# The first two slots' rows asked for ahead of q, k and v, and ten memsets instead of seven between indirect writes, in an attention and mixture-of-experts kernel

## The chip, the cores and the metric

The kernel runs on one core of one Trainium2 chip. The metric is device time in microseconds (us) of one execution; lower is better. A core has five instruction queues that run at the same time, each in its own order: TensorE (PE in the profile; its weight loads are listed as PEld), VectorE (DVE), ScalarE (ACT), GpSimd (POOL) and SyncE (SP). SP computes nothing here: it asks for transfers between the chip's memory and the core's. A request that has to wait holds up every request behind it on the same queue.

## The reference, cut to what matters

Dilated and sliding-window attention over 8 batches, 8 heads, 576 positions and 64 features, then a dropless mixture of 8 experts over the 4608 tokens that come out, each token going to the one expert with the largest logit.

```
scores = where(mask[h], q @ k.T / sqrt(64), -1e9)     # h < 4: 32 newest keys; h >= 4: every 4th of 128
x      = softmax(scores) @ v                          # (8, 8, 576, 64) -> (4608, 512)
e      = argmax(x @ w_gate);  gate = softmax(x @ w_gate)[e]
y      = gate * (relu(x @ w1[e]) @ w2[e])             # w1: 512 x 1024, w2: 1024 x 512, fp32
```

## The kernel before, in words

**Attention** goes through 16 pairs p (batch b = p // 2, head type ty = p % 2), two units each. For a pair SP loads q and k into a tile `raw` (3 buffers, `load_whole`, L379), DVE transposes them into `qT` and `kT` (L538, L549), and SP loads v into one of two tiles with a single buffer each: v0 for even pairs in one request (L405, shown as v_71 in the order), v1 for odd pairs in 13 requests (L429, v_72). A unit is then: PE `scores` (L595), DVE masking (L611) and row minimum (L623), ACT exponentials (L629), DVE reciprocal (L640, L642), POOL normalisation (L646), PE transposes `weights` (L657, three groups of three, over two small PSUM banks), ACT or DVE copies to `eT` (L878), PE `xo` (L676), and a copy to `xT`.

**Routing** of a batch b follows its two pairs. PE computes `lp` and `logits` (L976), DVE chooses the expert (`choose`, L988 to L994, which frees the bank that `logits` took), counts (`front`, L998), PE ranks (L1007, L1010), DVE makes the row numbers `idx` (L1022), PE and ACT or DVE turn x into token rows (`xrow` L939, `rows` L950), and POOL writes the rows into `bucket` in memory, sorted by expert, with five indirect writes (L493). After the batches 1, 2, 4 and 7 DVE also makes tables (L1142 and on) that tell which rows the next slots hold.

**Experts** work on slots of up to 128 rows of one expert. For slot j SP asks for the rows (`fetch_x`: four requests for `x`, L1379, and one for the gates `gt`, L1384), which waits until the writes of the batches so far have landed in `bucket`. It asks for the weights (`fetch_w`, L1401) only where the expert is another than two slots before. DVE transposes x to `xt` (L1407), PE runs the first layer `ph` (L1415, 8 pieces of 4 matmuls, 32 in all) and the second `py` (L1431, 8 matmuls), ACT and DVE evict (L1426, L1436), and POOL scatters the result to the output (L1456). Slots 0 and 1 can start after batch 1, slots 2 to 5 after batch 2. What is left over per expert goes through 14 small slots (`ph_s`, `h_s`, `py_s`, L1518 to L1545) near the end.

**The order** on all five engines is made by a planner before the program is built (class `Plan`). Each piece of work is a step with guessed durations, with steps it comes after, rings of buffers it takes, and a rank. The planner repeatedly takes, among the steps that could start within 0.25 of the earliest one, the one with the lowest rank, and appends its instructions to its engine. Where PE would idle in the attention part it puts in filler matmuls on a constant tile (L714, `<-idle`), as many as fit the idle time it expects. Between two indirect transfers that follow each other on POOL it puts IDLE one-column memsets of a tile that nobody reads (L722), and counts on 0.21 for each. The engines then run these fixed orders; only semaphores decide when.

Of the kernel before, what the change touches and what calls it, by code (L numbers as in the profile page):

```python
# [63 lines left out]
STEP_W = 1.0  # L64
ROUTE = 5.0

IDLE = 7

MOVED = 3.0
MOVED_S = 1.5  # L70
# [3 lines left out]
WHOLE = 14  # L74

QUADS = 4

BY_PE = 0
RUN, LONG = S * 4 // 128, S // 16
# [2 lines left out]
class Ring:  # L82


    def __init__(self, bufs):
        self.bufs, self.holds = bufs, []
# [19 lines left out]
class Step:  # L106
    def __init__(self, engines, us, emit, after, takes, uses, rank, moved, dense, slow, dmas):
        self.engines = (engines,) if isinstance(engines, str) else engines
        self.us = dict.fromkeys(self.engines, us) if isinstance(us, float) else us
        self.emit, self.after, self.rank, self.moved = emit, after, rank, moved  # L110
        self.slow, self.dmas = slow, dmas
        self.takes, self.uses = takes, [*takes, *uses]
        self.end, self.dense, self.on = None, dense, None
        for h in self.uses:
            h.left += 1


class Plan:
# [18 lines left out]

    APART = 0.21 * IDLE

# [66 lines left out]
    def write(self):  # L206
# [8 lines left out]
        while open_:  # L215
            found = []
            for s in open_:
                free = [h.ring.free_at() for h in s.takes]
                if None not in free:
                    found.append(min(  # L220
                        (self.could(s, free, e) for e in s.engines),
                        key=lambda f: f[0] + s.us[f[2]] + self.COSTS.get(f[2], 0.0),
                    ))
            soon = min(f[0] for f in found) + self.SOON
            at, _, e, s = min((f for f in found if f[0] <= soon), key=lambda f: (f[1], f[0]))
            if e == "PE" and self.fill and not self.filled(s):
                idle, cold = at - self.free[e] - self.SLACK, self.slowed(at) > 1.0
                us = self.FILL * self.slowed(self.free[e])
# [3 lines left out]
            if e == "PE":  # L232
                at = max(at, self.free[e])
# [95 lines left out]
def kernel(  # L329
# [11 lines left out]
    packed, at = _constants()  # L341
# [364 lines left out]
    def hold(name):  # L706
        return Hold(ring[name])
# [12 lines left out]
    def pass_time():  # L720
        for _ in range(IDLE):
            nc.gpsimd.memset(still, 0.0)  # L722
# [11 lines left out]
    def attention():  # L734
# [12 lines left out]
        for p, (b, ty) in enumerate(pairs):  # L747
# [60 lines left out]
            for n in range(0 if p < BY_PE else 2):  # L808
                for g in range(2 if p < WHOLE else 1):
# [10 lines left out]
                    )  # L820
            quad = p < QUADS
            for hp in range(2):
# [807 lines left out]
    def moe():  # L1630
# [10 lines left out]
        asked = {}  # L1641

        def ask(j):
            known, sent = slot_known[j]
            hx = hold("x") if j < SURE else None
            asked[j] = (
                add("SP", 3.5, lambda e: fetch_x(j), after=[known, *sent],
                    takes=[hx] if hx else (), rank=900.0 + j, moved=1.4, dmas=5),
                hx,
            )  # L1650

        for j in range(3):
            ask(j)
        for j in range(SURE):
            known, sent = slot_known[j]
            D = {}
# [181 lines left out]
```

## Time and profile before

| | us |
|---|---|
| median of 3 runs (lowest, highest) | 781.12 (780.31, 782.7) |
| the profiled execution, whole | 781.74 |
| its span, first to last instruction | 780.0 |
| PE busy in the span | 742.8 |
| POOL busy in the span | 193.5 |

The whole time of the profiled execution is 1.74 us above its span; that part lies outside of the instructions. The profiled execution is 0.62 us above the median of the runs. The rows of the trace further down show, for an engine, when a group of instructions started, how long it took, its line, operation, output and input, its count, and in brackets how long the engine sat idle just before and what ended that. A matmul in fp32 appears as two records in the trace, so that `x18` is nine filler matmuls, while the order counts instructions. For SP a row shows when requests were issued, not when they landed.

### The profile page before, as it was taken

The page shows a single profiled execution, that of the slowest core. Times are in us where ns is not written, and L with a number is a line of the kernel's source. Part 1 is how long each engine was busy: PE and PEld are TensorE (multiplying, and loading weights), DVE is VectorE, ACT ScalarE, POOL GpSimd, SP SyncE. Part 2 cuts the span into 40 slices and gives each one's busy share as a digit, 9 for nine tenths or more (in the row PEclk, how much of TensorE's full clock was granted, in tenths as well). Part 3 has the DMA queues.
Part 4 walks back from the last instruction along what each step waited for, and adds up shares of the span by engine and source line. Part 5 has one row for each costly group of instructions (what it writes and reads, how often), then busy time and mean ns, then how long its engine had stood idle before and what let it go on. Part 6 is the DMA issues. An engine that isn't in the chain of part 4 may idle for free.

```text
span 780.0 us, 21889 instructions
## 1 busy us (share of the span) xinstructions
PE 742.8 (95%) x8406; PEld 562.4 (72%) x8406; DVE 257.6 (33%) x718; ACT 265.2 (34%) x868; POOL 193.5 (25%) x641
## 2 busy tenths in 40 slices
PE   5879989999999999999999999999999999999996
PEld 5768878868787776776776776777776776766664
DVE  7958858678857740710000000000000000000000
ACT  2766756576747754211111111111111111111100
POOL 1314343425253434260100100211221111102101
PEclk9989999999999999999999999999999999999999
DMA  9878775969997979799629684727678166099660
GB/s 274 301 224 272 229 239 137 361 190 323 260 268 178 298 226 350 262 387 323 214 47 314 201 258 100 254 51 250 196 261 299 35 226 261 22 316 351 257 222 30
DMA packets 140399, 180.68 MB, mean 232 GB/s; under 512 B 68764, under 2 KB 90014, under 8 KB 139776
## 3 DMA queue, kind: packets, MB, share of 16 engines
q1 hardware_dynamic: 132864, 159.00, 64.1%
q0 software_dynamic: 6272, 19.43, 6.5%
q8 instruction: 68, 1.11, 0.6%
q10 hardware_dynamic: 1152, 0.78, 0.4%
q14 instruction: 43, 0.35, 0.1%
HBM read 252.03 MB, written 19.95 MB: 349 GB/s over the span
## 4 chain that ended last, share of the span: by engine, by line
PE 80%; issue 8%; DMA 6%; DVE 3%; ACT 2%; POOL 1%; SPq 0%; POOLq 0%; DVEq 0%; ACTq 0%
PE ph L1415 27%; PE py L1431 25%; PE scores L595 6%; PE xo L676 6%; PE weights L657 4%; DMA qT<-in_moe_w_dram 4%; PE py_s L1545 3%; PE ph_s L1518 3%; PE weights L714 3%; PE xrow L939 2%; PE lp L962 1%; DMA raw<-in_k_dram 1%; DMA x<-bucket 1%; PE logits L976 1%; ACT eT L878 1%
## 5 line engine op out<-in xcount | busy, mean ns | idle before, releaser
L1415 PEld LDWEIGHTS ph<-xt,w 128*128 128x128 f32 x2112 | 243.2, 192 | 15.7 <-issue 14.6
L1415 PE MATMUL ph<-xt,w 128*128 128x128 f32 x2112 | 252.5, 277 | 0.0
L1431 PE MATMUL py<-w,h 128*128 128x512 f32 x528 | 236.5, 594 | 0.6 <-ACT h L1426 0.6
L1431 PEld LDWEIGHTS py<-w,h 128*128 128x128 f32 x528 | 96.0, 190 | 101.3 <-issue 100.8
L629 ACT ACTIVATE e<-e,lo 128x96 f32<-128x96 f32 x288 | 103.5, 363 | 19.6 <-DVE lo L623 19.6
L1407 DVE STREAM_TRANSPOSE xt<-x 128x512 f32<-128x512 f32 x30 | 21.3, 711 | 243.7 <-PE ph L1415 240.4
L1456 POOL DMA_INDIRECT out_dram<-y,to x30 | 29.5, 984 | 251.7 <-ACT y L1436 249.2
L646 POOL TENSOR_TENSOR e<-e,rec 128x864 f32<-128x864 f32 x32 | 52.3, 1633 | 141.1 <-DVE rec L642 112.6
L1426 ACT ACTIVATE h<-ph 128x512 f32<-128x512 f32 x63 | 37.6, 597 | 142.6 <-PE ph L1415 141.8
L1436 ACT ACTIVATE y<-py,gt 128x512 f32<-128x512 f32 x30 | 20.6, 687 | 157.8 <-PE py L1431 150.3
L595 PE MATMUL scores<-kT,qT 32*64 32x96 f32 (+1 forms) x2160 | 56.2, 259 | 12.0 <-issue 7.4
L595 PEld LDWEIGHTS scores<-kT,qT 32*64 32x64 f32 (+1 forms) x2160 | 49.1, 139 | 18.5 <-issue 14.3
L722 POOL MEMSET still<- 128x1 f32 x504 | 51.4, 102 | 25.0
L629 ACT ACTIVATION_READ_ACCUMULATOR e<-e,lo 128x1 f32 x288 | 54.4, 189 | 0.0
L493 POOL DMA_INDIRECT bucket<-rows,idx x40 | 39.2, 980 | 60.9 <-issue 16.9
L676 PEld LDWEIGHTS xo<-eT,v 96*64 96x64 f32 x1280 | 40.9, 138 | 12.3 <-issue 4.5
L657 PE MATMUL weights<-cst,e 128*96 128x128 f32 x288 | 45.1, 282 | 4.5 <-ACT eT L878 2.1
L611 DVE SCALAR_TENSOR_TENSOR e<-scores,cst 128x384 f32<-128x384 f32 (+1 forms) x128 | 45.5, 395 | 10.0 <-PE scores L595 9.0
L676 PE MATMUL xo<-eT,v 96*64 96x64 f32 (+1 forms) x1280 | 45.9, 225 | 3.0 <-issue 2.6
L878 ACT COPY eT<-weights 96x384 f32<-96x384 f32 x88 | 39.9, 480 | 22.8 <-PE weights L657 16.1
L657 PEld LDWEIGHTS weights<-cst,e 128*96 128x96 f32 x288 | 30.2, 129 | 17.2 <-issue 6.8
L1511 DVE STREAM_TRANSPOSE own<-own 128x128 f32<-128x128 f32 x14 | 4.3, 304 | 99.3 <-DMA own<-bucket 99.3
(168 smaller groups left out, 566.5 us busy)
## 6 DMA issues: line engine op xcount, KB each, us to landing
w<-in_moe_w_dram SPq DMA_DIRECT2D x66, 2048.0 KB
raw<-in_moe_w_dram SPq DMA_DIRECT2D x42, 1024.0 KB
qT<-in_moe_w_dram SPq DMA_DIRECT2D x28, 512.0 KB
w<-in_moe_w_dram SPq DMA_DIRECT2D x8, 1024.0 KB
raw<-in_q_dram SPq DMA_DIRECT2D x14, 576.0 KB
raw<-in_k_dram SPq DMA_DIRECT2D x14, 576.0 KB
x<-bucket SPq DMA_DIRECT2D x120, 64.0 KB
v<-in_v_dram SPq DMA_DIRECT2D x7, 864.0 KB
```

The source lines that it names most:

```text
L493: nc.gpsimd.indirect_dma_start(out=bucket, out_offset=bass.IndirectOffsetOnAxis(ap=idx, axis=0), in_=rows, in_offset=None, bounds_check=NR ...
L595: nc.tensor.matmul(two[r][QB * half : QB * half + QB, KB * c : KB * c + KB], lhsT=qT[:, QB * n : QB * n + QB], rhs=kt[:, QB * n : QB * n + ...
L611: nc.vector.scalar_tensor_tensor(out=e[p, c0 : c0 + w], in0=sc[r][p, a : a + w], scalar=-SCALE, in1=m[p, a : a + w], op0=OP.mult, op1=OP.add,)
L629: nc.scalar.activation(out=ev[:, c], in_=ev[:, c], func=AF.Exp, bias=lo[:, c : c + 1], scale=-1.0, accum_out=den[:, c : c + 1],)
L646: nc.gpsimd.tensor_tensor(out=ev, in0=ev, in1=rec.unsqueeze(2).broadcast_to([128, NC, KB]), op=OP.mult)
L657: nc.tensor.transpose(tp[0:KB, c], ev[:, 3 * g + c], ident)
L676: nc.tensor.matmul(xo[DH * r : DH * r + DH, g, lo - half_s * g : hi - half_s * g], lhsT=v0[:, hd, n] if ty == 0 else v1[:, n, hd], rhs=eT[ ...
L722: nc.gpsimd.memset(still, 0.0)
L878: copier(e)(S_["eT"][:, 3 * g : 3 * g + 3], S_["w", g][0:KB, 0:3])
L1415: nc.tensor.matmul(ph[:, f % 4], lhsT=w1s[j % 2][:, c, 128 * f : 128 * f + 128], rhs=xt[:, c], start=c == 0, stop=c == 3,)
L1426: nc.scalar.activation(to, ph, AF.Relu)
L1431: nc.tensor.matmul(py, lhsT=h[:, f], rhs=w2s[j % 2][:, f], start=f == 0, stop=f == 7)
```

## The change

The constant IDLE goes from 7 to 10. A step has a new field `ahead`, zero by default. The two steps that ask for the rows of slots 0 and 1 get rank 0 (it was 900 and 901) and `ahead` = 6.0, and the planner subtracts `ahead` from a step's possible start when it looks for the earliest one and for those that are close to it. The start itself, and what a step waits for, are as before.

```diff
-IDLE = 7
+IDLE = 10
+AHEAD_X = 6.0
@@ class Step
+        self.ahead = 0.0
@@ Plan.write
-            soon = min(f[0] for f in found) + self.SOON
-            at, _, e, s = min((f for f in found if f[0] <= soon), key=lambda f: (f[1], f[0]))
+            soon = min(f[0] - f[3].ahead for f in found) + self.SOON
+            at, _, e, s = min((f for f in found if f[0] - f[3].ahead <= soon), key=lambda f: (f[1], f[0]))
@@ moe
         for j in range(3):
             ask(j)
+        for j in range(2):
+            asked[j][0].rank, asked[j][0].ahead = 0.0, AHEAD_X
```

Lines from `Plan` on move down by 3, those below `ask` by 5. Since a step's place depends on all before it, POOL's order differs from the first writes into `bucket` on, and the orders of the other engines from about 110 to 130 us of the trace on. In the whole program the memsets go from 72 groups of 7 (504) to 71 groups of 10 (710), and the filler matmuls from 133 to 123; the matmuls that the result needs are the same.

**SP, around the first rows.** After the weights of slot 0 (w_0_90 and w_0_92) SP has, before the change, q and k of pair 10, the 13 requests for v of pair 7, and then the rows of slot 0 (x_2081):

```order
L1401 DMA w_0_92<-in_moe_w_dram 128x8x512
L379 DMA raw<-in_q_dram 128x1152
L379 DMA raw<-in_k_dram 128x1152
L429 DMA v_72<-in_v_dram 64x4x64
...
L429 DMA v_72<-in_v_dram 96x4x64
L1375 TENSOR_LOAD basei
...
L1379 DMA x_2081<-bucket 32x4x128
```
With the change the rows and gates of slots 0 and 1 (x_1892 and gt_1893, gt_1924) come first, then v of pair 7, then q and k of pairs 10 and 11:

```order
L1404 DMA w_0_92<-in_moe_w_dram 128x8x512
L1378 TENSOR_LOAD basei
...
L1382 DMA x_1892<-bucket 32x4x128
...
L1387 DMA gt_1893<-bucket 128x2
...
L432 DMA v_72<-in_v_dram 64x4x64
...
L432 DMA v_72<-in_v_dram 96x4x64
L382 DMA raw<-in_q_dram 128x1152
L382 DMA raw<-in_k_dram 128x1152
```
The ten row requests of two slots moved past 13 requests for v and two for q and k, which now stand behind whatever these ten wait for.

**PE, in the routing of batch 2.** Before, behind the second `xrow` of batch 2 and a group of `weights`:

```order
L657 MATMUL weights<-cst,e 96x128 x6
L714 MATMUL weights<-idle 128x128 x9
L939 MATMUL xrow<-cst,xT_73 128x2x2x32 x4
L1007 MATMUL rank<-front,idle 128x48
L1010 MATMUL rank<-oh,cst 128x40
L676 MATMUL xo<-eT,v_71 64x64 x8
L676 MATMUL xo<-eT,v_71 64x32 x4
L676 MATMUL xo<-eT,v_71 64x64 x8
L714 MATMUL rank<-idle 128x128
L657 MATMUL weights<-cst,e 96x128 x3
L1415 MATMUL ph<-xt,w_0_90 128x128 x8
L657 MATMUL weights<-cst,e 96x128 x6
```
With the change, from the same place (w_0_90 is the first layer's weights of slot 0):

```order
L660 MATMUL weights<-cst,e 96x128 x6
L1418 MATMUL ph<-xt,w_0_90 128x128 x8
L942 MATMUL xrow<-cst,xT_73 128x2x2x32 x4
L1418 MATMUL ph<-xt,w_0_90 128x128 x4
L1010 MATMUL rank<-front,idle 128x48
L1013 MATMUL rank<-oh,cst 128x40
L679 MATMUL xo<-eT,v_71 64x64 x8
L679 MATMUL xo<-eT,v_71 64x32 x4
L679 MATMUL xo<-eT,v_71 64x64 x8
L1418 MATMUL ph<-xt,w_0_90 128x128 x8
L660 MATMUL weights<-cst,e 96x128 x6
L1418 MATMUL ph<-xt,w_0_90 128x128 x4
```
Nine fillers became two pieces of slot 0's first layer, a third piece stands ahead of the ranks, and the last filler became two more pieces.

**DVE, in the routing of batch 3.** Before, the transposition of slot 2's rows (x_2580) stands ahead of the choice of experts (`top`, `dl`):

```order
L611 SCALAR_TENSOR_TENSOR e<-scores,cst 64x96
L623 TENSOR_REDUCE lo<-e 128x9
L1407 STREAM_TRANSPOSE xt<-x_2580 128x4x4x32
L640 TENSOR_SCALAR den<-den 128x9
L642 RECIPROCAL rec<-den 128x9
L538 STREAM_TRANSPOSE qT<-raw 128x18x32
L538 STREAM_TRANSPOSE kT_70<-raw 128x18x32
L988 TENSOR_REDUCE top<-logits 128x5
L989 TENSOR_TENSOR dl<-logits,top 128x40
```
With the change it is gone from there:

```order
L614 SCALAR_TENSOR_TENSOR e<-scores,cst 64x96
L626 TENSOR_REDUCE lo<-e 128x9
L643 TENSOR_SCALAR den<-den 128x9
L645 RECIPROCAL rec<-den 128x9
L541 STREAM_TRANSPOSE qT<-raw 128x18x32
L541 STREAM_TRANSPOSE kT_70<-raw 128x18x32
L991 TENSOR_REDUCE top<-logits 128x5
L992 TENSOR_TENSOR dl<-logits,top 128x40
```
It (x_2815) now stands behind the row numbers `idx` of that batch and one masking:

```order
L1025 CAST idx<-dest 128x5
L614 SCALAR_TENSOR_TENSOR e<-scores,cst 128x384
...
L614 SCALAR_TENSOR_TENSOR e<-scores,cst 64x96
L1410 STREAM_TRANSPOSE xt<-x_2815 128x4x4x32
L626 TENSOR_REDUCE lo<-e 128x9
L552 STREAM_TRANSPOSE qT<-raw 128x5x32x2
```
So the choice of experts of batch 3 has no transfer of rows ahead of it any more. On POOL the five writes of batch 1 had three groups of memsets and then a normalisation between the fourth and the fifth; with the change the normalisation stands between the third and the fourth.

## Rows read from the trace of the kernel before

**Rows 1.** The page: the span, and busy time, share of the span and instructions of each engine.

```profile
span 780.0 us, 21889 instructions
PE 742.8 (95%) x8406; PEld 562.4 (72%) x8406; DVE 257.6 (33%) x718; ACT 265.2 (34%) x868; POOL 193.5 (25%) x641
```
**Rows 2.** The span cut into stretches. Columns: stretch, its length, then busy us and instructions of PE, PEld, DVE, ACT and POOL, the granted PE clock as a share of full speed, the busy share of the DMA engines, and GB/s.

```profile
136.00:190.00 54.00, 50.05 (x861) 41.92 (x862) 39.92 (x108) 35.08 (x138) 22.41 (x64) 1.00 0.88 282
190.00:300.00 110.00, 106.91 (x1575) 84.73 (x1574) 70.20 (x187) 72.28 (x264) 40.80 (x97) 1.00 0.90 261
300.00:550.00 250.00, 249.35 (x1803) 180.07 (x1804) 29.57 (x130) 41.59 (x71) 52.25 (x243) 1.00 0.68 224
550.00:745.00 195.00, 192.24 (x1804) 133.95 (x1804) 12.21 (x40) 30.04 (x60) 32.94 (x153) 1.00 0.66 230
```
**Rows 3.** PE in order of time, routing of batch 2 and the start of slot 0.

```profile
129.92 2.17 PE L714 MATMUL weights<-idle 128*128 128x128 f32 x18
132.46 0.66 PE L939 MATMUL xrow<-cst,xT 128*128 128x128 f32 x4 [0.37 <-ACT rows L950]
...
133.79 1.39 PE L676 MATMUL xo<-eT,v 96*64 96x64 f32 x40 [0.20 <-ACT rows L950]
135.48 0.49 PE L714 MATMUL rank<-idle 128*128 128x128 f32 x2 [0.31 <-issue]
136.14 0.53 PE L657 MATMUL weights<-cst,e 128*96 128x128 f32 x3 [0.17 <-issue]
136.51 1.95 PE L1415 MATMUL ph<-xt,w 128*128 128x128 f32 x16
```
**Rows 4.** SP's requests in order of time around the first rows.

```profile
108.25 0.52 SPq L1401 DMA_DIRECT2D w<-in_moe_w_dram  x2
117.63 0.35 SPq L379 DMA_DIRECT2D raw<-in_q_dram  x1
...
119.57 8.60 SPq L429 DMA_DIRECT2D v<-in_v_dram  x13
129.29 1.90 SPq L1379 DMA_DIRECT2D x<-bucket  x4
...
134.57 0.35 SPq L1384 DMA_DIRECT2D gt<-bucket  x1
```
**Rows 5.** DVE in order of time: the choice and count of batch 2, the transposition of slot 0's rows, and the first transposition of pair 10's q.

```profile
129.22 0.20 DVE L994 TENSOR_TENSOR oh<-cst,best 128x40 f32<-128x40 f32 x1
129.45 0.97 DVE L998 TENSOR_TENSOR front<-front,oh 128x8 f32<-128x8 f32 x5
...
134.68 0.71 DVE L1407 STREAM_TRANSPOSE xt<-x 128x512 f32<-128x512 f32 x1
...
159.27 1.24 DVE L538 STREAM_TRANSPOSE qT<-raw 128x576 f32<-128x576 f32 x1
```
**Rows 6.** POOL in order of time: the writes of batch 1 with memsets and the normalisation between them, and the last scatter of the program.

```profile
101.49 1.01 POOL L493 DMA_INDIRECT bucket<-rows,idx  x1 [8.97 <-DVE avail L1182]
102.50 1.05 POOL L722 MEMSET still<- 128x1 f32 x7
104.20 0.98 POOL L493 DMA_INDIRECT bucket<-rows,idx  x1 [0.65 <-issue]
...
110.55 1.65 POOL L646 TENSOR_TENSOR e<-e,rec 128x864 f32<-128x864 f32 x1
112.36 0.93 POOL L493 DMA_INDIRECT bucket<-rows,idx  x1 [0.17 <-issue]
...
774.85 0.98 POOL L1456 DMA_INDIRECT out_dram<-xT,rest_to  x1 [13.03 <-ACT xT L1436]
```
**Rows 7.** PE in order of time, logits of batch 3 and the `weights` behind them.

```profile
166.43 1.18 PE L976 MATMUL logits<-cst,ls 128*128 128x8 f32 x10
...
171.47 0.51 PE L657 MATMUL weights<-cst,e 128*96 128x128 f32 x3 [1.76 <-DVE dl L989]
...
174.83 0.32 PE L1007 MATMUL rank<-front,idle 128*128 128x48 f32 x2
```
**Rows 8.** DVE in order of time, the transposition of slot 2's rows and the choice of batch 3.

```profile
163.33 1.05 DVE L623 TENSOR_REDUCE lo<-e 128x9 f32<-128x864 f32 x1
167.65 0.71 DVE L1407 STREAM_TRANSPOSE xt<-x 128x512 f32<-128x512 f32 x1 [3.27 <-DMA x<-bucket]
...
171.13 0.20 DVE L989 TENSOR_TENSOR dl<-logits,top 128x40 f32<-128x40 f32 x1
```
**Rows 9.** SP's requests in order of time: first-layer weights and rows of slot 2, and v of pair 9.

```profile
150.88 7.18 SPq L1401 DMA_DIRECT2D w<-in_moe_w_dram  x1
159.42 1.93 SPq L1379 DMA_DIRECT2D x<-bucket  x4
...
168.24 8.08 SPq L429 DMA_DIRECT2D v<-in_v_dram  x13
```
**Rows 10.** Who PE waited for from 136 us to the end. Columns: waiter, what ended the wait, us in total, times, longest.

```profile
PE weights L657 <- DVE dl L989: 1.8, 1, 1.8
...
PE weights L657 <- ACT eT L878: 1.3, 3, 0.7
```
**Rows 11.** PE in order of time: the first and the second `xo` of pair 7, which read the v of rows 4.

```profile
145.29 1.39 PE L676 MATMUL xo<-eT,v 96*64 96x64 f32 x40
...
158.56 1.39 PE L676 MATMUL xo<-eT,v 96*64 96x64 f32 x40
```
## The prediction

> **What bounds the kernel now.** I read the page first: PE is busy 742.8 of 780.0 us, the next engine 265.2 [rows 1]. So PE sets the end, and a change can gain only by taking out PE's idle time or the fillers that hide idle time, and can lose only by making PE wait. Next I cut the span into stretches, to see where that time is [rows 2]. From 300 to 550 us PE idles 250.00 - 249.35 = 0.65 us, from 550 to 745 2.76 us: there the slots' matmuls follow each other with no room. From 136 to 190 us it idles 54.00 - 50.05 = 3.95 us, and from 190 to 300 3.09 us. Fillers count as busy, so the third view is PE in order of time where they end [rows 3]: the last ten stand at 129.92 us (18 records, nine matmuls) and at 135.48 us (two records, one matmul). After that no filler runs; from 136.51 us slot 0's first layer fills the gaps. The fourth view is the list of waits [rows 10]: the one wait of PE for DVE's choice of experts (`dl`) takes 1.8 us, three waits for copies to `eT` 1.3 us together. The change acts at 109 to 175 us; what PE gains there it keeps to the end if no new wait follows, because nothing behind it has slack to swallow it.
>
> **Fillers.** With the rows of slot 0 asked for earlier, nine fillers are replaced by two pieces of slot 0's first layer, and the tenth by two more. A filler costs 2.17 us / 9 = 0.24 us [rows 3], so ten cost 2.4 us. The pieces that stand in their place have to run anyway. This holds if `xt` of slot 0 is ready at 130 us. DVE's order puts it behind the choice of batch 2, which ends at 129.42, so it runs 129.45 to 130.16 (0.71 us, as it takes at 134.68) [rows 5], just when the `weights` ahead of the fillers end. Are the rows there? SP is free for them after 108.77 us (weights of slot 0, 108.25 + 0.52) [rows 4]. They wait for the five writes of batch 1 to land. These start 2.71 us apart with seven memsets (104.20 - 101.49); a memset is 1.05 / 7 = 0.15 us, so ten make that 3.16 us [rows 6]. With the normalisation (1.65 us) in the third gap, the writes start at 101.5, 104.65, 107.8, about 110.6 and 113.8 and the last ends at about 114.7, 1.4 us later than now (112.36 + 0.93). How long a write takes to land no row tells alone. From below it is nothing; from above it is 780.0 - 775.83 = 4.2 us, what lies between the end of the last scatter and the end of the span, with all that the program still does [rows 6]. I take the upper end: SP goes on at 118.9 us. Ten requests took 134.92 - 129.29 = 5.6 us [rows 4], so the rows are asked for by 124.5, and those of slot 0 by about 121.3. Slot 2's rows were transposed 6.3 us after their last request (159.42 + 1.93 to 167.65) [rows 8, 9], the slowest case at hand, which gives 127.6, ahead of 129.45. **Term: -2.4 us.**
>
> **Small idle times beside them.** PE idles 0.20, 0.31 and 0.17 us at 133.79, 135.48 and 136.14, and 0.37 us at 132.46 [rows 3]. Three pieces of `ph` now stand in front of the first three (one at the ranks, two behind `xo`), and a piece is 1.95 / 2 = 0.98 us, so they close. The 0.37 stays: two pieces end at about 132.1, and PE waits for ACT's copy as before. **Term: -0.7 us.**
>
> **The choice of batch 3.** Now DVE reaches `xt` of slot 2 at 164.38, waits 3.27 us for its rows, and only then goes on to `dl` at 171.13 [rows 8], while the logits are done at 167.6 [rows 7]. They hold one of two small banks, so `weights` wait 1.76 us at 171.47 [rows 7]. With the change this `xt` stands far behind the choice. DVE would have 164.38 us in place of 167.65 for the same work, so `dl` comes right when the logits end, and the wait goes. Where does the stall go? To the new place of `xt`, behind `idx` of batch 3 and a masking. SP now has v of pair 9 and q and k of pair 12 ahead of slot 2's rows. The 13 requests for v wait for the last reader of pair 7's v, `xo` at 158.56 [rows 11], which comes some 1.5 to 3 us earlier by the terms so far; add 8.08 us for them, some 0.8 us for q and k (0.35 each and the gap) and 2.3 us for the rows (1.93 + 0.35) [rows 4, 9], and the rows are asked for by about 168.5. They land between then and 174.8 (the 6.3 us above). DVE gets there at about 173.4, so it waits 1.4 us at worst, behind which stand the row minimum and exponentials of a unit whose `weights` are many PE pieces away. I take no cost, and keep 1.8 us for the range. **Term: -1.8 us.**
>
> The Trainium skill ("DMA: Bandwidth & Descriptors", section "Issuing engines are not separate DMA queues") says that all requests end up on the same 16 engines and interleave there whoever issued them. By its fixed and variable cost ("Anatomy of one DMA") 256 KB of rows would take 2.0 + 0.6 = 2.6 us, an estimate; the 6.3 us of [rows 8, 9] behind 2 MB of weights speak for the interleaving, and with 2.6 us DVE would not wait at all.
>
> **Costs.** 206 more memsets are 31 us of POOL time, but POOL is busy only 193.5 of 780.0 us [rows 1], and between 300 and 745 us it has 85 of 445 [rows 2]. What they delay is the last of five writes, by 4 x 0.45 = 1.8 us at most; the rows of the slots that need it are used tens of us later. If that cover were gone, 1.8 us per routed batch on the rows' way. q and k of pair 10 are asked for at about 131 in place of 117.63 [rows 4]; DVE first needs them at 159.27 [rows 5], so some 24 us stay. v of pair 7 is asked for from 124.5 in place of 119.57, its last request leaves at 133, and with 6.3 us it lands at 139.4, ahead of its `xo`, now at 145.29 [rows 11], then at about 143.5. The memsets' clock effect: PE is granted 1.00 of full speed, its 2.4 GHz level, from 136 us on [rows 2], and useful matmuls replace fillers, so I see none.
>
> The new order is not free of waits. It puts two groups of `weights` in a row where a piece of `ph` stood between them, and attention now runs 3 to 5 us earlier against the same ACT and DVE work. Waits of PE for `eT` are 1.3 us from 136 us on [rows 10]; nothing says that the new order has fewer. No row shows the new ones; from below nothing is added (1.3 even goes), from above the idle time of 136 to 190 us comes back whole, 3.95 us. I take as much again as is there now. **Term: +1.3 us.**
>
> **Sum.** -2.4 - 0.7 - 1.8 + 1.3 = -3.6 us. The profiled execution, 781.74, would take 778.1; the median of the runs shown is 0.62 lower, so 781.1 - 3.6 = **777.5 us**.
>
> **Rivals.**
> A, the stall of DVE only moves: slot 2's rows arrive late at the new place and PE pays the 1.8 us there. Then 779.3. For it: 3.27 us are lost to just this transfer now; against it: PE is not next in line behind the new place.
> B, attention can't run earlier: ACT and DVE are 65% and 74% busy from 136 to 190 us (35.08 and 39.92 of 54) [rows 2], and PE waits for them as much as it gained, the 3.95 us of idle time a second time. 777.5 - 1.3 + 3.95 = 780.2, within 0.3% of before. That the earlier rows are of no use at all ends there too, at 781.1.
> C, slower: SP is held at slot 0's rows. Everything for attention stands behind that wait, v of pair 7 first. By the row above v has 143.5 - 139.4 = 4.1 us of slack, when I already took 4.2 us for a write's landing. Each us of holding beyond that is a us of PE at `xo` of pair 7; with the 4.9 us that the first three terms gain it gets slower beyond 9 us, so from about 128 us as the time that SP goes on. At 131.5, 3.5 us later, the time is 784.6. For it: no row shows how long such a write takes to land; against it: SP would have to be held for more than 13 us after the last write was issued at 114.7.
> The Trainium skill states the rule behind C ("DMA: Bandwidth & Descriptors", "Anatomy of one DMA"): a semaphore wait happens on the issuing sequencer before dispatch. The trace agrees: rows 9 show v requested only after the rows ahead of it.
>
> **Chances and range.** The forecast and what lies near it 0.55, A 0.17, B 0.16, C 0.12. A time that can be told from no change is over 0.3% away, 2.3 us: below 778.8 or above 783.5. The forecast is faster by that, A and B are not; C is slower. With the spread of the unknown waits about the forecast and A: faster 0.58, same 0.29, slower 0.13. The range goes from all waits for `eT` gone, 777.5 - 2.6 = 774.9, to B's end, 781.2; C is left out. The likeliest case by itself spans 776.2 to 778.8.
>
> **What would show it.** Right: no filler after 125 us; PE at `ph` of slot 0 by 130.5; no PE wait for `dl` in the routing of batch 3; PE at the ranks of batch 3 some 4 us before 174.83 [rows 7] with three pieces of slot 1 ahead of them. Wrong: SP's first `x` request after 124 us; `xo` of pair 7 waiting for a transfer; DVE idle before `xt` of slot 2 and PE after it; waits for `eT` above 3 us from 130 us on.

## The result and the profile after

The changed kernel takes 789.81 us (median), the kernel before 783.44 beside it: ratio 1.007, 95% interval 1.0049 to 1.009. Two later comparisons gave 1.0047 (1.001 to 1.0084) and 1.0056 (1.0029 to 1.0084). It is slower by 0.5 to 0.7%, where 0.5% faster was forecast. Some executions of either kernel took over 1.5% more than its fastest one; the ratios leave these out, the medians do not. The profiled execution took 787.09 us, 5.35 us more than that of the kernel before.

Page and stretches of the changed kernel, columns as in [rows 1] and [rows 2]:

```profile
span 785.2 us, 22052 instructions
PE 748.2 (95%) x8386; PEld 566.6 (72%) x8386; DVE 256.7 (33%) x716; ACT 266.4 (34%) x870; POOL 214.3 (27%) x847
...
136.00:190.00 54.00, 49.10 (x824) 40.72 (x827) 38.50 (x110) 32.93 (x131) 23.44 (x78) 0.97 0.95 308
190.00:300.00 110.00, 108.36 (x1536) 83.90 (x1529) 70.69 (x180) 68.43 (x258) 40.20 (x113) 0.97 0.89 255
300.00:550.00 250.00, 247.28 (x1825) 178.71 (x1823) 30.68 (x138) 47.72 (x87) 64.04 (x335) 1.00 0.68 223
```

Against [rows 1, 2] PE is 5.4 us longer busy although ten fillers (2.4 us) are gone, while its idle time over the whole span is the same (785.2 - 748.2 = 37.0 us, it was 37.2). The granted clock is 0.97 instead of 1.00 from 136 to 300 us: some matmuls ran slowly. Idle time grew from 136 to 190 us (54.00 - 49.10 = 4.90, it was 3.95) and from 300 to 550 (2.72, it was 0.65). These are the two places to look at.

**First the gain, which is there.** The same `scores` of the kernel before and of the changed one show where each execution stood ahead of the change's first effect on PE:

```profile
124.33 1.88 PE L595 MATMUL scores<-kT,qT 32*64 32x96 f32 x72
```
```profile
126.11 1.88 PE L598 MATMUL scores<-kT,qT 32*64 32x96 f32 x72
...
131.95 2.05 PE L1418 MATMUL ph<-xt,w 128*128 128x128 f32 x16
...
170.19 2.84 PE L1418 MATMUL ph<-xt,w 128*128 128x128 f32 x24
172.87 0.32 PE L1010 MATMUL rank<-front,idle 128*128 128x48 f32 x2
```

This execution of the changed kernel is 1.78 us late before PE's order differs. That is not the change's doing: executions differ this early (in another one of the changed kernel the fillers that come at 117.44 before came at 118.08, here at 119.22), and here the clock was 0.91 from 60 to 80 us, where the kernel before had 1.00. Then slot 0's first layer runs where the fillers of [rows 3] ran, and the ranks of batch 3, with three more pieces of slot 1 ahead of them, come at 172.87 where they came at 174.83 [rows 7]: 3.7 us earlier once the late start is taken off. With the three pieces, 2.84 us, PE is some 6 us ahead in work: the ten fillers are gone, and PE's idle time between the `scores` above and these ranks fell from some 4.2 us to 0.8. SP asked for the first rows at 119.27 us.

**Then the loss.** SP, DVE and PE of the changed kernel around slot 2's rows, in order of time:

```profile
148.57 10.52 SPq L1404 DMA_DIRECT2D w<-in_moe_w_dram  x1
159.19 12.82 SPq L432 DMA_DIRECT2D v<-in_v_dram  x13
...
174.25 2.23 SPq L1382 DMA_DIRECT2D x<-bucket  x4
```
```profile
173.99 1.44 DVE L614 SCALAR_TENSOR_TENSOR e<-scores,cst 128x384 f32<-128x384 f32 x4
180.97 0.71 DVE L1410 STREAM_TRANSPOSE xt<-x 128x512 f32<-128x512 f32 x1 [5.54 <-DMA x<-bucket]
181.61 1.01 DVE L626 TENSOR_REDUCE lo<-e 128x9 f32<-128x864 f32 x1
182.54 1.38 DVE L552 STREAM_TRANSPOSE qT<-raw 128x320 f32<-128x320 f32 x2
183.95 0.55 DVE L881 COPY eT<-weights 96x384 f32<-96x384 f32 x1
```
```profile
184.65 0.51 PE L660 MATMUL weights<-cst,e 128*96 128x128 f32 x3 [3.69 <-DVE eT L881]
184.99 1.06 PE L1418 MATMUL ph<-xt,w 128*128 128x128 f32 x8
186.46 0.88 PE L660 MATMUL weights<-cst,e 128*96 128x128 f32 x3 [0.41 <-ACT eT L881]
187.26 2.40 PE L679 MATMUL xo<-eT,v 96*64 96x64 f32 x40
189.59 3.48 PE L598 MATMUL scores<-kT,qT 32*64 32x96 f32 x72
193.00 2.08 PE L1418 MATMUL ph<-xt,w 128*128 128x128 f32 x8
194.87 2.73 PE L1434 MATMUL py<-w,h 128*128 128x512 f32 x4
```

Read from the top: the weights and the 13 requests of v hold SP until 172, so slot 2's rows are asked for at 174.25 and are there at 180.97. DVE, whose order has `xt` next, stands for 5.54 us, and behind `xt` stand `lo`, `qT` and then the copy to `eT` that frees a bank for PE's `weights`. PE stands for 3.69 + 0.41 us, the longer of them for that copy. After that every matmul takes longer than the same form did a little earlier: `xo` 2.40 us for 1.39, `scores` 3.48 for 1.88, `ph` 2.08 for 1.06, `py` 2.73 for 1.88, `weights` 0.88 for 0.51. That is 1.01 + 1.60 + 1.02 + 0.85 + 0.37 = 4.9 us. The granted clock in 4 us stretches (columns: stretch, length, PE busy and records, granted clock, DMA share, GB/s) says why:

```profile
180.00:184.00 4.00, 0.96 (x9) 1.00 0.98 300
184.00:188.00 4.00, 2.94 (x28) 0.79 1.08 359
188.00:192.00 4.00, 4.00 (x92) 0.50 1.04 322
192.00:196.00 4.00, 4.00 (x30) 0.50 0.73 215
196.00:200.00 4.00, 4.00 (x43) 0.93 0.98 217
```

PE was busy 0.96 of 4 us, and then the clock is at 0.50, the 1.2 GHz level, for some 10 us. In this execution the stall costs 4.1 us of waiting and 4.9 us of slow matmuls, 9.0 together: more than the early gain.

**Two later waits**, SP and PE of the changed kernel:

```profile
354.12 1.81 SPq L1510 DMA_DIRECT2D raw<-in_moe_w_dram  x3
356.27 1.08 SPq L1510 DMA_DIRECT2D qT<-in_moe_w_dram  x2
358.92 2.10 SPq L1404 DMA_DIRECT2D w<-in_moe_w_dram  x1
```
```profile
376.59 7.38 PE L1418 MATMUL ph<-xt,w 128*128 128x128 f32 x64 [1.78 <-DMA w<-in_moe_w_dram]
...
551.10 0.43 PE L1548 MATMUL py_s<-qT,own 128*32 128x128 f32 x8 [1.76 <-DMA qT<-in_moe_w_dram]
```

The new order asks for the 4 MB of weights of the first small slot (`raw` and `qT`) ahead of slot 9's first weights, and PE waits for the latter at 376.59; the small slot's weights are first read at 404.78. At 551 PE waits for the second weights of the fourth small slot. The kernel before waited at neither place.

### The profile page after: what moved, and what is told of

Same layout as the page of the kernel before. It is cut to its first block, busy times and chain, and to the rows that moved or that the text cites. A ratio compares the mean times of both kernels' runs of the same rounds, so it can differ in the third digit from the quotient of the medians.

```text
span 785.2 us, 22052 instructions
## 1 busy us (share of the span) xinstructions
PE 748.2 (95%) x8386; PEld 566.6 (72%) x8386; DVE 256.7 (33%) x716; ACT 266.4 (34%) x870; POOL 214.3 (27%) x847
## 4 chain that ended last, share of the span: by engine, by line
PE 80%; issue 8%; DMA 5%; DVE 3%; ACT 2%; SPq 1%; POOL 1%; POOLq 0%; DVEq 0%; ACTq 0%
PE ph L1418 25%; PE py L1434 24%; PE scores L598 6%; PE xo L679 6%; PE weights L660 4%; PE py_s L1548 3%; PE ph_s L1521 3%; PE weights L717 3%; DMA w<-in_moe_w_dram 2%; PE xrow L942 2%; DMA qT<-in_moe_w_dram 1%; PE lp L965 1%; PE logits L979 1%; DMA raw<-in_k_dram 1%; ACT e L632 1%
## 5 line engine op out<-in xcount | busy, mean ns | idle before, releaser
L725 POOL MEMSET still<- 128x1 f32 x710 | 72.1, 102 | 36.9
L679 PEld LDWEIGHTS xo<-eT,v 96*64 96x64 f32 x1280 | 42.7, 144 | 15.9 <-issue 9.5
L679 PE MATMUL xo<-eT,v 96*64 96x64 f32 (+1 forms) x1280 | 47.7, 231 | 5.4 <-issue 5.2
L626 DVE TENSOR_REDUCE lo<-e 128x9 f32<-128x864 f32 x32 | 33.2, 1037 | 0.7
```

Source lines behind the costliest of these rows:

```text
L679: nc.tensor.matmul(xo[DH * r : DH * r + DH, g, lo - half_s * g : hi - half_s * g], lhsT=v0[:, hd, n] if ty == 0 else v1[:, n, hd], rhs=eT[ ...
```

## Experiments

The theories: **1**, slot 2's rows are asked for too late, DVE stops, PE stops, the clock falls; **2**, the ten memsets cost; **3**, the later waits cost. Where only a place in the order is changed, the planner's finished list is kept and single steps are moved in it before it is emitted. In the diffs `x2` is the request for the rows of slot 2, `xt2` its transposition, `v9` the 13 requests of pair 9's v, `short0` the weights of the first small slot, `weights18.0` PE's step that waited 3.69 us. The clock in the table is the mean over the executions that enter the ratio.

| kernel | us | before beside it | ratio (95%) | mean granted clock, before's |
|---|---|---|---|---|
| changed, again (after_again) | 787.74 | 782.98 | 1.0047 (1.001, 1.0084) | 0.983, 0.988 |
| changed, again (after_2) | 787.42 | 782.63 | 1.0056 (1.0029, 1.0084) | 0.983, 0.990 |
| xt2_later | 787.58 | 782.98 | 1.0054 (1.0022, 1.0086) | 0.979, 0.988 |
| x2_sooner | 787.48 | 782.98 | 1.0052 (1.0023, 1.0081) | 0.979, 0.988 |
| fill_stall | 785.37 | 782.98 | 1.0034 (1.0004, 1.0065) | 0.986, 0.988 |
| x23_sooner | 777.65 | 780.66 | 0.996 (0.9926, 0.9994) | 0.985, 0.986 |
| short0_later | 785.75 | 780.66 | 1.0034 (0.999, 1.0078) | 0.983, 0.986 |
| x23_short0 | 779.11 | 782.41 | 0.9965 (0.9934, 0.9996) | 0.987, 0.989 |
| late_two | 781.48 | 782.63 | 1.000 (0.9971, 1.0028) | 0.986, 0.990 |
| all_four | 773.43 | 780.66 | 0.9905 (0.9859, 0.9951) | 0.989, 0.986 |
| all_four_2 | 775.2 | 782.63 | 0.9926 (0.9893, 0.996) | 0.989, 0.990 |
| before_ten | 777.43 | 780.66 | 0.9971 (0.994, 1.0002) | 0.988, 0.986 |
| idle10 | 783.24 | 782.41 | 1.0003 (0.9975, 1.003) | 0.987, 0.989 |
| ahead7 | 778.02 | 782.41 | 0.9933 (0.991, 0.9955) | 0.987, 0.989 |
| ahead7_2 | 777.69 | 780.26 | 0.9935 (0.9897, 0.9974) | 0.986, 0.987 |
| ahead7_x23 | 777.5 | 782.63 | 0.9945 (0.9915, 0.9974) | 0.988, 0.990 |
| ahead7_x23_2 | 774.29 | 780.26 | 0.9911 (0.9881, 0.9942) | 0.988, 0.987 |
| before_xt2_later | 779.08 | 782.41 | 0.9969 (0.9943, 0.9996) | 0.991, 0.989 |

### The changed kernel again

> The changed kernel itself, as the yardstick for the runs beside it. Its trace had DVE waiting 5.54 us for the rows of slot 2 (asked for at 174.25, behind the 13 requests of v of pair 9, 12.82 us long), PE waiting 3.69 + 0.41 us from 184.65 for the eT copy behind that wait, and then the granted clock at 0.79, 0.50, 0.50 and 0.93 in the four stretches of 4 us from 184 to 200. All theories expect the same place again: a DVE wait of 4 to 6 us, a PE wait of 3 to 4.5 us, the clock below 0.9 for some 10 us, and a time 4 to 7 us above the kernel before (ratio 1.005 to 1.009).

> The changed kernel again, as the first corner of a square of four kernels on one chip: 4 to 7 us over the kernel before (ratio 1.004 to 1.009), with DVE's wait for slot 2's rows of 5 us, PE's wait of 4 us near 184, and PE's waits of 2 us or more at 372 and 547.

Both came out as expected in time. PE waited 3.74 us in the one trace and 4.00 in the other at this place. The clock behind it was low for some 3.5 us in the first (after_again, columns as above) and for 10 us again in the second:

```profile
184.00:188.00 4.00, 4.00 (x51) 0.58 1.07 340
188.00:192.00 4.00, 4.00 (x87) 1.00 1.03 321
```

Seven traces have this wait, 3.12 to 5.49 us long: the three of the changed kernel, and those of short0_later, late_two, ahead7 and ahead7_2 below. In each the clock fell behind it. So the wait comes with the order, and its cost in clock varies. Over the executions the mean granted clock is 0.005 to 0.006 under that of the kernel before; 0.0055 of 787 us is 4.3 us, an estimate, nearly the whole difference of 4.8.

### One move at the early stall: xt2_later, x2_sooner

```diff
+        self.later("xt2", "DVE", 4)      # xt2_later
```


> The changed kernel, with the conversion xt of slot 2 taken four steps later in DVE's order (behind lo, the qT eviction, the eT copy and a masking); SP's order stays. Theory 1 (the late rows of slot 2 stop DVE, DVE stops PE, and the stop costs the granted clock as well): the eT copy comes some 5 us earlier, PE's 4.1 us of waits and the 4.8 us of matmuls at the lower clock both go, and the time is 7 to 9 us under the changed kernel, 2 to 4 us under the kernel before. Theory 2 (the ten memsets between the indirect writes are what costs): nothing is won, within 0.3% of the changed kernel. Theory 3 (the loss is spread over the later order, weight loads after 300 us included): 3 us are won at most and the time stays above the kernel before.

```diff
+        self.ahead_of("x2", "v9")        # x2_sooner
```


> The changed kernel, with the request for the rows of slot 2 put ahead of the 13 requests of v of pair 9 in SP's order; DVE's order stays. Theory 1 with the late request as its cause: the rows are asked for by 160 to 162 rather than 174.25, land by 168, DVE's 5.54 us wait goes, with it PE's 4.1 us and the lower clock: 7 to 9 us under the changed kernel. If it was not the request but the rows' own transfer (slow beside the weights), the DVE wait stays at 3 us or more and little is won. v of pair 9 goes out 2 to 3 us later; if that is missed, PE waits for it instead at the attention of pair 9. Theories 2 and 3: within 3 us of the changed kernel.

Neither won anything, so theory 1's number failed for one move. The traces show why. DVE and SP of x2_sooner:

```profile
171.56 0.71 DVE L1443 STREAM_TRANSPOSE xt<-x 128x512 f32<-128x512 f32 x1
...
187.83 0.71 DVE L1443 STREAM_TRANSPOSE xt<-x 128x512 f32<-128x512 f32 x1 [4.26 <-DMA x<-bucket]
```
```profile
172.71 0.32 SPq L1437 DMA_DIRECT2D w<-in_moe_w_dram  x1
173.85 4.62 SPq L1415 DMA_DIRECT2D x<-bucket  x4
```

Slot 2's rows now come in time, and DVE stands 4.26 us at the next slot's, asked for behind a 2 MB weight load: 9.4 us from the last of the four requests (173.85 + 4.62) to their use. The Trainium skill ("DMA: Bandwidth & Descriptors", section "Issuing engines are not separate DMA queues") says that transfers interleave on the same 16 engines; this gap, against 6.3 us in [rows 8, 9], fits that, though it does not show that the two were served in turns: rows served only after the weights would be late as well. In xt2_later that same wait is 2.97 us. Granted clock and PE of x2_sooner, columns as above:

```profile
188.00:192.00 4.00, 2.03 (x22) 0.80 0.76 225
192.00:196.00 4.00, 4.00 (x75) 0.50 0.55 135
...
200.00:204.00 4.00, 4.00 (x68) 0.50 1.06 406
```

PE's longest wait is now 1.64 us instead of 3.69, and the clock is low for longer, from 191 to 207. In the trace of xt2_later no wait of PE between 165 and 230 us is longer than 0.4 us, and the clock fell all the same:

```profile
188.00:192.00 4.00, 3.48 (x51) 1.00 0.99 369
192.00:196.00 4.00, 3.63 (x86) 0.73 0.50 119
196.00:200.00 4.00, 4.00 (x75) 0.50 1.05 227
```

The mean clock fell to 0.979 in both kernels. So the wait was won (some 2 us in x2_sooner, 4 in xt2_later) and about as much was lost in clock.

### The wait without the idle PE: fill_stall

```diff
+        self.fillers("weights18.0", 15)
```


> The changed kernel, with 15 filler matmuls (0.24 us each, 3.6 us in all) in PE's order just ahead of the score-times-v group that waited 3.69 us; nothing else is moved. It tells the wait from the clock. If the lower clock followed from the idle wait, the wait itself is only covered by work that nobody needs, PE is as late as before at the group, but the clock stays at 1.00 behind it: 4 to 5 us under the changed kernel, within 2 us of the kernel before. If the clock fell for another reason (what PE had done before 184, or nothing of this place), the slow stretch stays and the time stays within 1 us of the changed kernel.

```profile
180.83 3.51 PE L745 MATMUL weights<-idle 128*128 128x128 f32 x30
185.05 0.51 PE L688 MATMUL weights<-cst,e 128*96 128x128 f32 x3 [0.71 <-DVE eT L912]
```
```profile
180.00:184.00 4.00, 4.00 (x38) 1.00 1.00 304
184.00:188.00 4.00, 2.89 (x42) 1.00 1.08 357
188.00:192.00 4.00, 3.71 (x103) 1.00 1.03 347
```

PE gets past the group at 185.05, as late as before, and the clock stays at 1.00 where it fell in all seven traces with the wait: at this place the low clock followed from the idle PE, as far as one trace shows. The times are 2.4 us under the changed kernel, half of what was expected and within the intervals of the two, so they do not show it: the mean clock rose by 0.003, which is 2.3 us. In this trace the later waits were 3.10 and 2.8 us (0.54 + 0.58 + 1.70), with the clock between 0.84 and 0.95 in the 8 us stretches about them.

### Both requests at the early stall: x23_sooner

```diff
+        self.ahead_of("x2", "v9")
+        self.ahead_of("x3", "v9")
```


> The changed kernel, with the requests for the rows of slots 2 and 3 both put ahead of the 13 requests of v of pair 9 in SP's order. With slot 2's request alone moved, DVE's wait went from xt of slot 2 (5.54 us, now none) to xt of slot 3 (4.26 us at 187.83), whose request stood behind a 2 MB weight load; PE then waited 1.64 us at 190.72 and the clock fell to 0.50 from 191 to 207. Theory 1 (rows asked for too late, DVE, PE, then the clock): with both moved there is no DVE wait over 2 us for rows and no PE wait over 1 us between 168 and 210, the clock stays at 1.00 there, and the time is 6 to 9 us under the changed kernel, 781 to 777. Theory 3 (the later stretch: PE's wait for the weights of slot 9 at 372 of 1.8 to 3.1 us, and for the second weights of a short slot at 547 of 1.8 to 3.2 us, with the clock near 0.8 behind each): those waits stay or grow by what PE is earlier, and the time stays within 3 us of the changed kernel.

DVE's waits for the rows of slots 2 and 3 are gone, and the kernel is 0.4% faster than before, where the changed one is 0.5 to 0.7% slower: 7 to 8 us won, as expected. Theory 1 holds for the place, with two requests late rather than one. Not as expected: PE still waited 1.28 us at 194 with the clock at 0.50 behind it, and the waits at 367 (2.33 us) and 545 (0.78 + 2.39) stayed, as theory 3 said.

### The later waits: short0_later, x23_short0, late_two, all_four

```diff
+        self.later("short0", "SP", 4)    # short0_later
```


> The changed kernel, with the 4 MB of weights of the first short slot asked for behind the next two slots' weights (four requests later in SP's order), instead of ahead of the first weights of slot 9. Nothing else moves. In the trace of the changed kernel SP waited 6.6 us for the plan of the short slots, asked for these 4 MB at 354.12, for slot 9's first weights at 358.92, and PE waited 1.78 us for them at 376.59 (2.44 and 3.1 us in the runs since), with the granted clock at 0.79 to 0.84 behind it; the 4 MB are first used near 405. Theory 3: that wait goes, 2 to 5 us under the changed kernel. Theory 1: the wait goes as well, but it is paid at the next limit (the wait at 547 grows by as much), under 1.5 us won.

```diff
+        self.ahead_of("x2", "v9")        # x23_short0
+        self.ahead_of("x3", "v9")
+        self.later("short0", "SP", 4)
```


> The changed kernel with three of the four places put right: the rows of slots 2 and 3 ahead of v of pair 9 and the first short slot's weights behind the next two slots' weights; the fourth short slot's weights stay behind the fetch of rows that nothing needs yet. It tells what the fourth place is worth: with all four the kernel took 773.4 us (0.9905 of before), with the first two 777.7 (0.996). If the wait at 547 is set by the order at that place, PE waits 2 us or more there again and the time is 2 to 4 us over that of all four; if it came from the 372 wait's place, the wait is under 1 us and the time is that of all four.

Moving the first small slot's weights takes the wait at 372 away (1.06 and 0.86 us are left at a later place) but wins 1 to 2 us by itself and nothing beside the early repair: intervals that overlap with the kernels without it. The wait at 547 stands in both (2.69 and 0.77 + 2.31 us) and pays part of it back.

```diff
+        self.later("short0", "SP", 4)    # late_two; all_four has x2 and x3 ahead of v9 as well
+        self.behind("short3", "SP")      # the fetch of rows ahead of short3 goes behind it
```


> The changed kernel with only the two later places of SP's order put right: the first short slot's weights behind the next two slots' weights, and the fourth short slot's weights ahead of the fetch of rows that nothing needs yet. The early stall near 184 is left. If the two losses add, this is 4 to 7 us under the changed kernel (the waits at 372 and 547, some 5 us, and the lower clock behind them) and about as far over the kernel with all four places put right. If the later waits only take back what is won early (a limit of the transfers), nothing is won here, since the early stall already costs it.

> The changed kernel with four places of SP's order put right: the rows of slots 2 and 3 asked for ahead of v of pair 9, the first short slot's weights behind those of the next two slots, and the fourth short slot's weights ahead of one fetch of rows that nothing needs yet. All the planner's other decisions stay. If theories 1 and 3 together are the whole loss, no PE wait over 1 us is left between 60 and 725, the granted clock is 1.00 from 70 on, and what is left is the early gain: 5 to 7 us under the kernel before, 774 to 778. If a limit of the transfers stands behind the later waits, one of them (372 or 547) stays at 2 us or more and the time is 780 to 785.

> The changed kernel with all four places of SP's order put right, as the last corner of the square: 0.986 to 0.995 of the kernel before, no PE wait over 1.2 us between 60 and 715. If the losses add, it is as far under late_two as the early repair alone was under the changed kernel (7 to 9 us).

These make the square. Changed kernel 1.0058 (the mean of three), early place alone 0.996, later places alone 1.000, all four 0.9915 (the mean of two). In us of a kernel of 782: the early place is worth 7.6, the later ones 4.5, both together 11.2, each good to some 3 us by the intervals, so within them the losses add. On one chip, with the kernels beside each other (after_2, late_two, all_four_2), the later places won 5.9 us and the early one 6.3 more, where 4 to 7 and 7 to 9 were expected. All waits of PE over 1.2 us are gone in all_four; these are its longest from 125 us on (columns as in [rows 10]) and what the clock, not 1.00 as expected, did after the first:

```profile
PE scores L634 <- issue: 1.1, 1, 1.1
PE py L1475 <- DMA w<-in_moe_w_dram: 1.0, 1, 1.0
```
```profile
192.00:196.00 4.00, 3.52 (x66) 0.75 0.30 73
196.00:200.00 4.00, 4.00 (x23) 0.83 1.07 241
```

With four requests moved, the change is 0.7 to 1% faster than the kernel before. That is more than the forecast of -3.6 us.

### The memsets: before_ten, idle10

```diff
-        for _ in range(IDLE):
+        for _ in range(10):              # before_ten: the order planned with 7, ten memsets in it
```


> The kernel before, every instruction in its order, but ten memsets instead of seven between two of POOL's indirect writes where the program puts them. It measures the second half of the change without the new order. Theory 2 (the memsets cost): the writes of a batch come up to 3 x 0.07 us x 20 later, the places of the last batches with them, and some of the loss of 4 to 6 us shows here: 784 to 789. Theories 1 and 3: the writes' end has slack, within 0.3% of the kernel before (781 to 785).

```diff
-IDLE = 7
+IDLE = 10                                # idle10: nothing else of the change, planned anew
```


> The kernel before with ten memsets, planned anew: the second half of the change alone. Its SP order keeps slot 2's rows ahead of v of pair 9. Theories 1 and 3: no stall over 3 us near 170 to 200, and a time within 0.5% of the kernel before (the ten memsets alone, in the order of before, gave 0.997). Theory 2: slower than before by 0.3% to 1%.

Theory 2 falls for these two orders: ten memsets in the old order cost nothing and may win a little, though the memsets of a gap take 1.53 us instead of 1.05, more than the expectation's 3 x 0.07 us more; planned anew they make no difference. The trace of idle10 has a stall that was not expected, 4.49 us of PE waiting for DVE's `rows` at 174.82: it is another order with its own weak place.

### The requests: ahead7

```diff
-IDLE = 10
+IDLE = 7                                 # ahead7: the changed kernel with seven memsets, planned anew
```


> The changed kernel with seven memsets again, planned anew: the first half of the change alone. Its SP order has v of pair 9 ahead of the rows of slot 2, slot 3's rows behind a weight load, and the first short slot's weights ahead of slot 9's, as in the changed kernel; the fourth short slot's weights have nothing extra ahead of them. Theory 1 and 3 (the requests put behind others): the stalls near 184 and 372 are there again, the one at 547 is under 1 us, and it is as slow as the changed kernel or up to 4 us faster (ratio to before 1.001 to 1.008). Theory 2 (memsets): the kernel before or better.

> The first half of the change alone again (seven memsets, planned anew). If the early stall costs wait and clock here too: PE stopped 3 to 4 us near 184 with the clock under 0.9 behind it, and a time 4 to 8 us over the same kernel with the rows of slots 2 and 3 asked for sooner. If something later sets the pace of this kernel, the stall is there and the time is within 1.5 us of the other's.

```diff
+        self.ahead_of("x2", "v9")        # ahead7_x23: ahead7 with both requests moved
+        self.ahead_of("x3", "v9")
```


> The first half of the change alone (seven memsets, planned anew; it took 0.993 of the kernel before, with PE stopped 3.1 us at 183.6 and the clock at 0.57 behind it, and no wait at 372 or 547), with the rows of slots 2 and 3 asked for ahead of v of pair 9. If the early stall costs its wait and the lower clock behind it, 6 to 9 us go: 0.982 to 0.986 of the kernel before. If what is won is taken back at the weights of a later slot, a wait of 2 us or more shows there and 0 to 4 us are won.

> The first half of the change alone with the rows of slots 2 and 3 asked for ahead of v of pair 9, again. If the early stall costs wait and clock: 4 to 8 us under the kernel beside it, 0.983 to 0.989 of the kernel before. If something later sets the pace: within 1.5 us of it, with small waits of PE in other places (1.2 us at 197, 1.4 us at 218 in its first trace).

The first half of the change alone is 0.65% faster than before, where theories 1 and 3 expected 0.1 to 0.8% slower; theory 2 had this right. It has the early stall (3.12 and 5.49 us of PE waiting in its two traces) and neither later wait. The changed kernel's order with seven memsets was not run, but the memsets themselves are not what costs: all_four has ten, ahead7_x23 has seven, no wait of PE in their traces is over 1.4 us, and they are alike (means 0.9915 and 0.9928). So the change loses with both halves together, by an order that neither half gives. Of the 9.7 us between ahead7 and the changed kernel the later waits explain 4.5; the rest is not explained. And the early repair, worth 7.6 us above, won nothing here by the first comparison (0.9933 to 0.9945) and 0.24% by the second, beside each other (0.9935 to 0.9911), within the intervals. In the two traces beside each other, ahead7_2 and ahead7_x23_2, PE's longest waits are:

```profile
181.36 0.84 PE L660 MATMUL weights<-cst,e 128*96 128x128 f32 x3 [5.49 <-DVE eT L881]
```
```profile
195.04 1.53 PE L632 MATMUL scores<-kT,qT 32*64 32x96 f32 x51 [1.11 <-issue]
...
221.61 0.34 PE L713 MATMUL xo<-eT,v 96*64 96x64 f32 x4 [1.09 <-DMA v<-in_v_dram]
```

The 5.49 us are gone and 2.2 us of other waits have come, the second for a v, with the clock at 0.68 from 224 to 232. Why 7.6 us there are 0 to 2 here is open.

### The stall of the kernel before: before_xt2_later

```diff
+        self.later("xt2", "DVE", 5)
```


> The kernel before, with the conversion xt of slot 2 taken five steps later in DVE's order, behind the choice of batch 3; nothing else moves. It prices the stall of before (DVE 3.27 us on the rows of slot 2, PE 1.76 us on the choice behind it; 2.78 us in the run with ten memsets, with the clock at 0.80 behind it). By the trace of before alone (no lower clock there) 1.8 us are won; if such a stall costs the clock in some executions, 2 to 5 us; if something else ends the choice late, nothing.

2.4 us won (0.9969; the interval goes from 0.3 to 4.5 us), too wide to tell the 1.8 us of the trace from the 2 to 5 with the clock; PE's wait for `dl` of [rows 10] is gone.

## Why the prediction was wrong

**Fillers and small idle times: right.** No filler runs behind 121 us, `ph` of slot 0 is at 131.95 (130.2 without the late start, against 130.5). The first `x` request at 119.27 against 118.9 is luck: the last write of batch 1 ended at 117.39, not 114.7, in this late execution, and landed within 1.9 us, not the 4.2 taken.

**Choice of batch 3: right in itself.** PE does not wait for `dl`, the ranks come 3.7 us earlier against "some 4", with the three pieces ahead of them. Taken alone in the kernel before, this stall is worth 2.4 us against the term's 1.8.

**Where the stall goes: the step that failed.** The text asks "Where does the stall go?", puts the rows' request at "about 168.5", lets DVE wait "1.4 us at worst" and says "I take no cost". Of its sizes one was far off: the 13 requests of v took 12.82 us, not the 8.08 of [rows 9] (11.7 to 12.6 in the other six traces with this wait). The last of the four requests was out at 176.5 (174.25 + 2.23), 8.0 us after the 168.5. Of that, 4.7 us are the requests of v; 1.9 are their start at 159.19, right behind a weight request of 10.52 us, and nearly all of these 1.9 are this execution's late start; 1.4 are q, k and the rows. Why the 13 requests took longer is open. The rows were there 4.5 us later, sooner than the 6.3 assumed. DVE reached `xt` at 175.4, not 173.4, again by the late start, and waited 5.54 us. And `weights` were not "many PE pieces away": three steps behind `xt` DVE had the copy to `eT` that PE needed. So two of the signs that the text named for being wrong came: DVE idle before `xt` of slot 2 with PE after it, and waits for `eT` above 3 us.

The 2.6 us that the prediction works out for these rows go by a cost that the Trainium skill ("DMA: Bandwidth & Descriptors", section "Anatomy of one DMA") gives for requests issued by GpSimd; these come from SP. The time of landing was not what mattered: even with 2.6 us the rows would have been there at 179.1 and DVE would have waited some 3.7 us.

**Rival A was this mechanism, at a fifth of its price.** It took the 1.8 us of the old stall; the new one measured 4.1 us of waiting and 4.9 us of slow matmuls in the profiled execution. The text says of the clock "so I see none": it looked at what the memsets and fillers do to it, not at what a wait of PE does. In [rows 2] the old wait of 1.76 us had left the clock at 1.00, and no longer wait was priced.

**The later waits were in no term.** "Nothing behind it has slack to swallow it" is true of PE, but the sum looked only at 109 to 175 us. The planner had made a new order for the whole program; its requests near 354 and 536 us were in the order and were not read against the times at which PE needs them. They are worth some 4.5 us by the runs above.

**Term for `eT`:** the waits for `eT` came to 4.3 us from 125 us on against the +1.3, but not by the term's reason, a shortage of time on ACT and DVE: 3.69 us of them are the wait for slot 2's rows passed on, and the others are 0.6. Rivals B and C did not happen: attention ran earlier, and SP was not held beyond 119.27. The kernel came out slower, but not by C, the only slower case that the text had.

## What to carry to other kernels

When a transfer is asked for sooner, look at the requests that now stand ahead of the next ones: a queue's order is a sum, and what steps back is paid for at the first engine that has no other work behind its wait. A new plan has to be read to the end of the program, not only around the steps that were touched. A wait of the engine that bounds the kernel should be priced with the clock behind it, by runs and not by one trace, since behind the same wait the clock was low for 3.5 us in one execution and for 10 us in another. And a repair is worth what its own order makes of it: the same two requests moved won 7.6 us in one order and 0 to 2 in another.

## What the runs showed of the hardware

The clock did not follow the length of the wait. After 3.69 us it was at 0.50 for some 10 us in one execution of the changed kernel and after 3.74 us for some 3.5 us in another. In x2_sooner it was low for 16 us after waits of 1.64 and 0.17 us, with PE busy without a break from 192 on; in xt2_later it was at 0.50 from 196 to 204 us with no wait above 0.4 us near it; in the kernel before, 1.76 us of waiting left it at 1.00, while in before_ten, after 2.78 us at the same place, it was 0.60 from 172 to 176 us. What decides this no run here settles. A single request could hold SP for 10.52 us (the weights at 148.57; 7.18 in [rows 9]), and 13 requests took 12.82 us here and 8.08 there, so here the time at which a later one went out could not be had by adding the durations of another trace.
